# Seven quarter products for the second layer of one more piece, with GpSimd as a second choice for the sums of weights and x

## The chip, the cores and the metric

The kernel runs on one core of a Trainium2 chip. The metric is the device time of one execution in microseconds, as the median of several runs. A TensorE clock of 1.00 in a row of the profile is the full 2.4 GHz.

## The reference

Eight batches of eight heads attend over 576 tokens of 64 columns, under a mask that lets a block of 64 tokens see itself and earlier blocks. The result, seen as 4608 rows of 512 columns, goes through a feed-forward network with a hidden width of 2048.

```python
scores = scale * np.matmul(q, k.transpose(0, 1, 3, 2))
scores = np.where(block_i >= block_j, scores, -1e9)
attn = softmax(scores)
x = matmul(attn, v), as (4608, 512)
h = x @ w_in
g = h * np.clip(h + 3.0, 0.0, 6.0) / 6.0
return (g @ w_out).astype(np.float32)
```

## The kernel before

The 4608 rows are cut into 13 pieces, numbered 0 to 12; a late piece is 384 rows. A piece goes through the first layer in 16 steps of 128 hidden columns and then through the second layer. Attention of the pairs of heads that fill a piece comes before it; the last pairs (28 to 31) fill pieces 10 to 12.

Numbers are split into a high and a low 16-bit half, and a product of two such numbers takes three 16-bit products (high by high, high by low, low by high). Each matmul is done in two halves of 64 weight columns that run side by side; so the second layer of a 384-row piece is, for each of 16 hidden steps and each of 3 row tiles, 6 matmuls of 512 columns (`ffn2_`, tiles `g` and `o`).

In place of eight quarter products, a matrix product can be made of seven, if sums of quarters of both operands are formed first and the products are summed in a fixed way at the end. `STR = (10, 11, 12)` names the pieces whose first layer is done so: `w_comb` forms the sums of w_in (tiles `wr`, `wq`, result `ws`), `x_comb` those of x (tiles `xr`, `xt`), and `h_pair` makes the seven products of two hidden steps (a pair, `c` = 0 to 7, PSUM tile `m`) and adds them to `hf` by VectorE and ScalarE. `SO = (11, 12)` names the pieces whose second layer is done so as well: `t_comb` forms the sums of w_out (tiles `tr`, `tw`; results in places that `t_homes` lists), `g_pair` applies the activation and forms the four sums of g (tile `rs`; 16-bit results `gr`, `gs`), and `o_pair` makes the seven products into six PSUM banks; at the end 14 additions by VectorE form the output rows (`osb`). A product of `o_pair` is 6 matmuls of 256 columns and 6 of 128.

For a piece in `SO` the products of the first layer have only two PSUM banks (the pool `ps_h`) after the first two pairs of `SO[0]`; a piece in `STR` alone takes three of five from another pool (`bank` in `h_pair`).

The instructions are recorded first (`Recorder.add`), some of them with several engines to choose from. `ORDER`, a packed table, then gives the order of all steps and the engine of each; each engine works through its own list in that order, and waits where an operand isn't ready. `SLOTS` tells which buffer of a pool a tile takes. In the kernel before, the sums of g and w_out may be made by VectorE or GpSimd, those in `w_comb` and `x_comb` by VectorE alone, but for the additions of the two 16-bit halves (`plus`).

Line 423 of the profile is the helper that emits every step, so that rows are told apart by their tiles.

Of the kernel before, what the change touches and what calls it, by code (L numbers as in the profile page):

```python
# [56 lines left out]
SO = (11, 12)  # L57
# [1883 lines left out]
```

## Time and profile before

| | |
|---|---|
| median of 3 runs | 951.19 us (949.94 to 953.29) |
| profiled execution | 951.95 us, span 950.2 us |
| instructions | 34711 |
| TensorE busy | 942.8 us, 99% of the span |
| VectorE busy | 860.0 us, 91% |
| ScalarE busy | 722.0 us, 76% |
| GpSimd busy | 98.3 us, 10% |
| mean granted clock | 0.999 |

The time of an execution is the span and 1.75 us around it. Busy shares are means over the whole execution; stages differ. Durations in rows are those of single instructions, and neighbours on an engine overlap a little, so that a sum of durations is more than the busy time. A busy TensorE is not necessarily at its peak rate, since matmuls are pipelined: what a matmul costs in a stream is read from the distance between starts.

### The profile page before, as it was taken

The numbers are of one execution on the slowest core, as the hardware profiler recorded it, in microseconds if no ns is written. First come the engines' busy times: TensorE is split into PE (matmuls) and PEld (weight loads), VectorE is DVE, ScalarE is ACT, GpSimd is POOL, SyncE is SP. The second block draws the span as 40 slices with busy tenths as digits, with TensorE's granted clock in tenths as the row PEclk, the third lists the DMA queues.
The fourth block names the chain that finished last, engine by engine and source line by source line (L and its number), as shares of the span: only waits on it lengthen the run. The fifth ranks groups of instructions, "written<-read, shape, count | busy, mean of one in ns | idle before, by whom it ended". The sixth has DMA issues, their size and how long they took to land.

```text
span 950.2 us, 34711 instructions
## 1 busy us (share of the span) xinstructions
PE 942.8 (99%) x14108; PEld 686.3 (72%) x14108; DVE 860.0 (91%) x2526; ACT 722.0 (76%) x1791; POOL 98.3 (10%) x283
## 2 busy tenths in 40 slices
PE   9999999999999999999999999999999999999998
PEld 7777777766677766666667666666666667789998
DVE  5988999999999999999999999999899998999987
ACT  6989898888988878888788878778665356676662
POOL 1443101100000000110000010100000102000000
PEclk9999999999999999999999999999999999999999
DMA  7877699989999999999999899986785000000001
GB/s 211 280 246 213 125 178 169 180 166 181 167 189 168 179 188 162 183 189 181 165 201 181 169 165 180 179 162 121 127 128 106 2 2 36 2 35 4 14 26 36
DMA packets 390704, 132.93 MB, mean 140 GB/s; under 512 B 373264, under 2 KB 376592, under 8 KB 390544
## 3 DMA queue, kind: packets, MB, share of 16 engines
q1 hardware_dynamic: 389456, 129.87, 71.7%
q8 instruction: 110, 1.80, 0.8%
q10 hardware_dynamic: 1088, 0.85, 0.3%
q14 instruction: 50, 0.41, 0.1%
HBM read 45.09 MB, written 9.44 MB: 57 GB/s over the span
## 4 chain that ended last, share of the span: by engine, by line
PE 97%; DMA 1%; DVE 1%; ACT 0%; issue 0%; SPq 0%; DVEq 0%
PE o L423 37%; PE h L423 30%; PE m L423 9%; PE s L423 7%; PE pv L423 6%; PE pf L423 1%; PE sf L423 1%; PE pt L423 1%; DMA qkT<-qks 1%; PE pr L423 1%; PE gm L423 0%; DMA qf<-in_q_dram 0%; PE warm L423 0%; PE o_1b L423 0%; PE o_2b L423 0%; PE o_0b L423 0%
## 5 line engine op out<-in xcount | busy, mean ns | idle before, releaser
L423 PE MATMUL o<-wout,g 128*64 128x512 f16 (+2 forms) x2760 | 346.5, 378 | 0.0
L423 PE MATMUL h<-x,win 128*64 128x384 f16 (+2 forms) x3568 | 330.1, 318 | 0.0
L423 PEld LDWEIGHTS <-win 128*64 128x64 f16 (+1 forms) x4432 | 231.7, 110 | 81.3 <-issue 1.7
L423 PEld LDWEIGHTS <-g 128*64 128x64 f16 x2784 | 154.0, 110 | 98.6
L423 DVE SCALAR_TENSOR_TENSOR phl<-p,st,phl 128x64 f16<-128x64 f32 (+4 forms) x364 | 154.9, 447 | 4.2 <-ACT phl L423 2.3
L423 ACT ACTIVATE p<-p,st 128x192 f32<-128x192 f32 (+8 forms) x252 | 139.1, 553 | 22.7 <-DVE st L423 20.7
L423 DVE CUSTOM_DVE_ANT_0 p<-s,none,esc 128x64 f32<-128x64 f32 (+7 forms) x252 | 119.9, 486 | 14.6 <-PE s L423 11.2
L423 ACT ACTIVATE r<-h,eg,sh 128x384 f32<-128x384 f32 (+1 forms) x176 | 101.5, 591 | 40.2 <-PE h L423 33.9
L423 ACT ACTIVATE phl<-p,st 128x512 f16<-128x512 f32 (+5 forms) x173 | 97.2, 582 | 11.2 <-DVE st L423 6.1
L423 PE MATMUL s<-qkT 128*64 128x512 f16 (+7 forms) x1120 | 98.5, 287 | 0.8 <-DMA qkT<-qks 0.8
L423 DVE SCALAR_TENSOR_TENSOR g<-r,g 128x384 f16<-128x384 f32 (+1 forms) x160 | 86.2, 546 | 3.8 <-ACT g L423 3.0
L423 DVE SCALAR_TENSOR_TENSOR r<-r,eg,h 128x384 f32<-128x384 f32 (+1 forms) x144 | 84.2, 586 | 5.8 <-ACT r L423 4.5
L423 ACT ACTIVATE g<-r 128x384 f16<-128x384 f32 (+1 forms) x117 | 58.3, 503 | 18.2 <-PE o L423 11.3
L423 PEld LDWEIGHTS <-qkT 128*64 128x64 f16 x1120 | 53.4, 110 | 25.1 <-DMA qkT<-qks 1.0
L423 PEld LDWEIGHTS <-vhl 128*64 128x64 f16 x1344 | 58.4, 110 | 13.4
L423 PE MATMUL pv<-pT,vhl 128*64 128x192 f16 (+2 forms) x1344 | 67.2, 233 | 0.0
L423 ACT ACTIVATE hf<-m 128x192 f32<-128x192 f32 x90 | 28.5, 327 | 36.9 <-PE m L423 31.9
L423 PEld LDWEIGHTS <-ws 128*64 128x64 f16 x1152 | 52.0, 110 | 4.1
L423 ACT ACTIVATION_READ_ACCUMULATOR p<-p,st 128x1 f32 x252 | 47.7, 189 | 0.0
L423 DVE SCALAR_TENSOR_TENSOR qks<-qk,rs_q,qks 128x576 f16<-128x576 f32 x56 | 46.8, 838 | 0.9 <-ACT qks L423 0.6
L423 PE MATMUL m<-x,ws 128*64 128x192 f16 x864 | 46.8, 246 | 0.0
L423 PE MATMUL m<-x,win 128*64 128x192 f16 x768 | 41.4, 246 | 0.4 <-DVE hf L423 0.4
(229 smaller groups left out, 1414.1 us busy)
## 6 DMA issues: line engine op xcount, KB each, us to landing
vx<-vhl SPq DMA_DIRECT2D x56, 160.0 KB, 3.4
vnat<-in_v_dram SPq DMA_DIRECT2D x63, 128.0 KB, 3.5
qk<-in_k_dram SPq DMA_DIRECT2D x28, 288.0 KB, 4.4
qk<-in_q_dram SPq DMA_DIRECT2D x28, 288.0 KB, 3.9
out_dram<-osb SPq DMA_DIRECT2D x29, 256.0 KB, 2.8
rawo<-in_moe_w_out_dram SPq DMA_DIRECT2D x13, 512.0 KB, 4.9
x<-in_moe_w_in_dram SPq DMA_DIRECT2D x9, 512.0 KB, 5.5
rawi<-in_moe_w_in_dram SPq DMA_DIRECT2D x6, 512.0 KB, 4.8
```

The lines of the kernel that those rows point to most:

```text
L423: getattr(eng, method)(*args, **kw)
```

## The change

Piece 10 joins `SO`. So its 288 matmuls of 512 columns in the second layer become 672 (8 pairs, 7 products, 6 matmuls of 256 columns and 6 of 128), its activation goes through `g_pair`, its products of the first layer have two PSUM banks from the third pair on, its outputs are summed by 14 additions of VectorE, and `t_comb` comes before piece 10 in place of piece 11. Since part of the place for the sums of w_out is still in use then (x of piece 10 lies in `vall`), nine of the twelve blocks that lay there move into longer `ws` tiles. The subtractions in `w_comb` and `x_comb` may now be made by GpSimd, and `wr` is made in two halves of 512 columns. The order table and the slot table are new; the order is as before up to the attention of pair 26, where TensorE is in the second layer of piece 7.

```diff
-SO = (11, 12)
+SO = (10, 11, 12)
...
+    def minus(out, a, b):
+        nc.add([(e, "tensor_tensor", (out, a, b), dict(op=ALU.subtract)) for e in ("vector", "gpsimd")])
+
     def w_comb(c):
-        r = attp.tile([P, NDT, NH], F32, tag="qks", bufs=1, name=f"wr{c}")
-        plus(r, win[:, c, :, 0], win[:, c, :, 1])
+        wr = [ffp.tile([P, 2, NH], F32, tag="stage", bufs=NST_B, name=f"wr{c}_{j}") for j in range(2)]
+        for j, r in enumerate(wr):
+            plus(r, win[:, c, 2 * j:2 * j + 2, 0], win[:, c, 2 * j:2 * j + 2, 1])
...
-        nc.vector.tensor_add(o[:, 0], a21, a22)
-        nc.vector.tensor_sub(o[:, 1], o[:, 0], a11)
-        nc.vector.tensor_sub(o[:, 2], a11, a21)
-        nc.vector.tensor_sub(o[:, 3], a12, o[:, 1])
+        plus(o[:, 0], a21, a22)
+        minus(o[:, 1], o[:, 0], a11)
+        minus(o[:, 2], a11, a21)
+        minus(o[:, 3], a12, o[:, 1])
...
-        t = pool.tile([P, 4, 2, 2, P], F16, tag=tag, bufs=bufs, name=f"ws{c}")
+        nu = 2 if tag in ("qkT", "pT2") else 1 if tag == "pT01" else 0
+        t = pool.tile([P, 8 * 2 * P + nu * 2 * DM // 2], F16, tag=tag, bufs=bufs, name=f"ws{c}")
+        more[c] = t[:, 8 * 2 * P:].rearrange("p (i l n) -> p i l n", i=nu, l=2) if nu else None
...
     def x_comb(pc):
-            nc.vector.tensor_sub(t1, b12, b11)
-            nc.vector.tensor_sub(t2, b22, t1)
-            nc.vector.tensor_sub(t3, b22, b12)
-            nc.vector.tensor_sub(t4, b21, t2)
+            minus(t1, b12, b11)
+            minus(t2, b22, t1)
+            minus(t3, b22, b12)
+            minus(t4, b21, t2)
...
     def t_homes():
-        va = vall.rearrange("p v j h d -> p (v j h d)").bitcast(F16)[:, :4 * 3 * 2 * NM]
-        va = va.rearrange("p (c i l n) -> p c i l n", c=4, i=3, l=2)
+        va = vall.rearrange("p v j h d -> p (v j h d)").bitcast(F16)[:, :3 * 2 * NM]
+        va = va.rearrange("p (i l n) -> p i l n", i=3, l=2)
-        rest += [[va[:, i]] for i in range(4)]
+        rest += [[more[3], more[5]], [more[4], va[:, :1]], [more[6], va[:, 1:2]], [more[7], va[:, 2:]]]
```

In `ffn_step` the block that calls `t_comb` stands after the one that calls `x_comb` and `w_comb`.

How the table moves the work shows at two places. The first is the list of GpSimd behind the attention. In a row, the operation stands with its output, an arrow and its inputs; `rs10_2` is the sum tile of pair 2 of piece 10. Before, these are all the sums that GpSimd makes, for pieces 10 to 12 together:

```order
L423 TENSOR_TENSOR xr10_2_2229<-x2_83 128x384
L423 TENSOR_TENSOR xr10_1_2232<-x2_83 128x384
L423 TENSOR_TENSOR wr2_2242<-win_85 128x1024
L423 TENSOR_TENSOR xr11_2_2353<-x3_84 128x384
L423 TENSOR_TENSOR wr7_2257<-win_85 128x1024
L423 TENSOR_TENSOR tw0_2330<-tr0_0_2328 128x256
L423 TENSOR_TENSOR tw0_2330<-tr0_1_2329,tr0_0_2328 128x256
L423 TENSOR_TENSOR tr1_0_2331<-wout_86 128x512
L423 TENSOR_TENSOR rs12_3_2469<-hf12_3_2466 128x192
L423 TENSOR_TENSOR rs12_3_2469<-rs12_3_2469,hf12_3_2466 128x192
```

After, two pairs of piece 10 alone:

```order
L427 TENSOR_TENSOR rs10_2_2324<-hf10_2_2315 128x192 x2
L427 TENSOR_TENSOR tw4_2286<-tr4_0_2284 128x256
L427 TENSOR_TENSOR tw4_2286<-tr4_1_2285,tr4_0_2284 128x256
L427 TENSOR_TENSOR tw4_2286<-tr4_1_2285,tw4_2286 128x256
L427 TENSOR_TENSOR rs10_2_2324<-rs10_2_2324,hf10_2_2315 128x192
L427 TENSOR_TENSOR rs10_2_2324<-hf10_2_2315,rs10_2_2324 128x192
L427 TENSOR_TENSOR tw4_2286<-tr4_1_2285,tw4_2286 128x256
L427 TENSOR_TENSOR rs10_3_2331<-rs10_3_2331,hf10_3_2328 128x192
```

Ten sums of GpSimd have become 146, and 64 of them stand between the first sums of piece 10 and the first of piece 11; none of the sums that add the two halves of w_in, w_out or x (`wr`, `tr`, `xr`) is left there.

The second place is VectorE's list at the sums of g. Before, in piece 11, where the sums of w_out were still made:

```order
L423 TENSOR_TENSOR rs11_3_2395<-hf11_3_2392 128x192
L423 SCALAR_TENSOR_TENSOR hf11_4_2399<-rs11_4_2402,eg8_698,hf11_4_2399 128x768
L423 TENSOR_TENSOR tw5_2345<-tr5_1_2344,tw5_2345 128x256
L423 TENSOR_TENSOR rs11_4_2402<-hf11_4_2399 128x192
L423 SCALAR_TENSOR_TENSOR gs11_3_1_2398<-rs11_3_2395,gs11_3_1_2398 128x384
L423 SCALAR_TENSOR_TENSOR gr11_4_2403<-hf11_4_2399,gr11_4_2403 128x576
L423 TENSOR_TENSOR tw5_2345<-tr5_1_2344,tw5_2345 128x256
L423 SCALAR_TENSOR_TENSOR gs11_3_0_2397<-rs11_3_2395,gs11_3_0_2397 128x384
```

After, in piece 10, where that now falls:

```order
L427 TENSOR_TENSOR hf10_3_2328<-m10_3_7_2329,hf10_3_2328 128x192
L427 SCALAR_TENSOR_TENSOR gs10_1_0_2313<-rs10_1_2311,gs10_1_0_2313 128x384
L427 TENSOR_TENSOR hf10_3_2328<-m10_3_8_2330,hf10_3_2328 128x192
L427 SCALAR_TENSOR_TENSOR gs10_1_1_2314<-rs10_1_2311,gs10_1_1_2314 128x384
L427 TENSOR_TENSOR win_85<-tw4_2286,win_85 128x2x128
L427 TENSOR_TENSOR tr5_0_2287<-wout_86 128x512
L427 SCALAR_TENSOR_TENSOR hf10_3_2328<-rs10_3_2331,eg8_698,hf10_3_2328 128x768
L427 TENSOR_TENSOR ws3_2251<-tw4_2286,ws3_2251 128x2x256
L427 TENSOR_TENSOR rs10_3_2331<-hf10_3_2328 128x192
```

The sums themselves (`rs`, `tw`) are gone from VectorE but for one; the residuals that wait for them (`gs`, `win`, `ws`) stay, and now wait for GpSimd.

## Rows read from the trace of the kernel before

**Rows 1.** The page, busy time, share of the span and instructions of each engine.
```profile
PE 942.8 (99%) x14108; PEld 686.3 (72%) x14108; DVE 860.0 (91%) x2526; ACT 722.0 (76%) x1791; POOL 98.3 (10%) x283
```
**Rows 2.** The page, chain of work that ended last, share of the span by engine.
```profile
PE 97%; DMA 1%; DVE 1%; ACT 0%; issue 0%; SPq 0%; DVEq 0%
```
**Rows 3.** Waits of TensorE: waiting and releasing work, us in total, times, longest.
```profile
PE m L423 <- DVE hf L423: 0.4, 1, 0.4
```
**Rows 4.** Chain that ended last: start us, us, work, count of matmuls.
```profile
729.48 3.88 PE o L423 x36
...
764.27 1.95 PE h L423 x24
...
775.52 1.98 PE m L423 x48
...
931.80 14.02 PE o L423 x336
```
**Rows 5.** TensorE's timeline, second layer of piece 11: start us, us, operation, count.
```profile
869.86 0.36 PE L423 MATMUL o<-win,gs 128*64 128x128 f16 x6
870.03 0.36 PE L423 MATMUL o<-wout,gr 128*64 128x128 f16 x6
...
871.51 0.85 PE L423 MATMUL o<-vnat,gs 128*64 128x256 f16 x12
872.17 0.69 PE L423 MATMUL m<-x,ws 128*64 128x192 f16 x12
```
**Rows 6.** Stretch 860 to 880: us, busy PE, PEld, DVE, ACT, POOL, clock, DMA, GB/s.
```profile
860.00:880.00 20.00, 20.00 (x485) 19.85 (x481) 19.14 (x45) 13.51 (x29) 0.00 (x0) 1.00 0.02 4
```
**Rows 7.** VectorE by form, 700 to 950: count, busy us, mean ns of one, idle before.
```profile
L423 DVE TENSOR_TENSOR hf<-m,hf 128x192 f32<-128x192 f32 x72 | 24.5, 353 | 10.0 <-PE m L423 7.5 <-ACT hf L423 1.3 <-ACT gs L423 0.5
L423 DVE SCALAR_TENSOR_TENSOR g<-r,g 128x384 f16<-128x384 f32 x35 | 20.9, 605 | 1.5 <-ACT g L423 1.3
L423 DVE SCALAR_TENSOR_TENSOR gs<-rs,gs 128x384 f16<-128x384 f32 x32 | 17.6, 552 | 0.1
L423 DVE SCALAR_TENSOR_TENSOR hf<-rs,eg,hf 128x768 f32<-128x768 f32 x16 | 16.2, 1015 | 0.4 <-ACT rs L423 0.4
L423 DVE SCALAR_TENSOR_TENSOR gr<-hf,gr 128x576 f16<-128x576 f32 x16 | 12.0, 752 | 0.0
L423 DVE TENSOR_TENSOR ws<-wq,ws 128x1024 f16<-128x1024 f32 x8 | 10.8, 1354 | 1.4 <-ACT ws L423 1.4
L423 DVE TENSOR_TENSOR tr<-wout 128x512 f32<-128x512 f16 x15 | 10.2, 686 | 0.0
L423 DVE TENSOR_TENSOR wq<-wr 128x256 f32<-128x256 f32 x16 | 6.6, 419 | 0.1
```
**Rows 8.** VectorE's timeline from 743 to 745: start us, us, operation.
```profile
743.19 0.62 DVE L423 SCALAR_TENSOR_TENSOR r<-r,eg,h 128x384 f32<-128x384 f32 x1
743.72 0.35 DVE L423 SCALAR_TENSOR_TENSOR x<-pv,x 128x192 f16<-128x192 f32 x1
743.99 0.42 DVE L423 TENSOR_TENSOR wq<-wr 128x256 f32<-128x256 f32 x1
...
744.71 2.37 DVE L423 SCALAR_TENSOR_TENSOR g<-r,g 128x384 f16<-128x384 f32 x1
```
**Rows 9.** GpSimd's timeline from 640 on, sums only: start us, us, operation.
```profile
744.49 2.18 POOL L423 TENSOR_TENSOR wr<-win 128x1024 f32<-128x1024 f16 x1 [13.52 <-DVE wq L423]
...
796.78 1.58 POOL L423 TENSOR_TENSOR tw<-tr 128x256 f32<-128x256 f32 x1 [8.34 <-DVE ws L423]
798.32 0.73 POOL L423 TENSOR_TENSOR tw<-tr,tr 128x256 f32<-128x256 f32 x1
...
911.20 0.71 POOL L423 TENSOR_TENSOR rs<-hf 128x192 f32<-128x192 f32 x1 [110.86 <-DVE hf L423]
911.99 0.60 POOL L423 TENSOR_TENSOR rs<-rs,hf 128x192 f32<-128x192 f32 x1
```
**Rows 10.** VectorE's timeline beside the sum at 798.32: start us, us, operation.
```profile
798.40 0.93 DVE L423 TENSOR_TENSOR tw<-tr,tw 128x256 f32<-128x256 f32 x1 [0.62 <-POOL tw L423]
```

More of the change, by code (lines that the diff above doesn't have):

```diff
@@ new lines @@
+    "p4IhxXHv^{rKGOupEdg+ZS(G`+?zM{)At>E`!4OkhV3>-@7%p@Yj=Ff+QTQ-&6#`a9~Srh_m3S0XU{$SHR;d!d-or_H#|mpH2H{)"
+    "^#$_hi(jS~eZAUnZOfId+n)cmHNKSb?Zfr-%QmBZUc7weyL8#|*WPb_5=j05c%nyO=8$<GF&2Kdo|bm@4xj8qVu>UDq}5}u;UlF("
+    "6B8J+z+q1I&hc(k6Q)Z#&D1@v>GY{HC52B14W9ZWIE%-bpYco-lx!v`6^|;Ll&xKv*&H%CLRU0}Un~%^S+3kMV~>Ql)Q(HZiySe2"
+    "!mOlJ)z#d^`2|72OVV<p)DzpIr>#0LJ0|wHW==!Xbm_I$wx!MG6`^OtLPD1<-_UV==dRs1PE=OO&BHpoSI8B;UDX>m?eD9pn>^#i"
+    "-1?rzmoxi`r#IJIo;;=a{b%Z#gYzCWTs(U0@!!wq&R@9n<msWqQ~upFFuWZ9^~(HbMql2}h=2Zi!JfU!Z?E31S>3ZXA+fe@o$;;p"
@@ new lines @@
+    "7AB^R^zCnceq?Ohx@E_AvmZ$<zhrJqmwhBkYumKj?eE=LR#@|UpFD<mjvnfO!<Uo|`Y_Ycxpb1(tUGsyj~G1i{wNIG5gjW!ov8h@"
+    "AE?f*T-BSKx6mJopp_4cOJMu1_VEi)YY1fPU42&*lZGXy<nO*#P?$V_Ph`{rZP(HC>9N-rEj*ri<JgIcw4$uavHYqD<Ht?ZZMwW="
+    "Yc{94rg-y}h!NjX_wLL1&WpKtX^iWdwL2bmpIW#6<hJN1-2Ff1@PD38J$UHM&bjjrANlqB&)@AMZ}V>6db{Y|oedlR-OagGw&dRZ"
+    "_YWREdK|IXh>>mm;YQA+DXv_$U}^5qyg?3*gNH;itpkQRIX^w1Ft8CUV_o)*64r`@`2~gM;!%^IxkxychIF^1Sv8>;>apd|O=+^v"
+    "I4iRk7FhgnKMw-&=Evh-KDlp-9_>xC8E^a5lYBKG@Z~G7;XbjA^J8B72ff)`CtWyU;>j__!69LGV=4Aq#>H)DN@-EAdcS(j+BVHB"
@@ new lines @@
+    "leBcZ=Bc;u)Nh?O{qD{TKc#A0QTgjD>oTt{IB{=%NyYt#r_Y={w;}vd<(0=(t$!P;H?}`{dj6lmu4i&x))2!7Mwkn`J2Lkfcg{BM"
+    "GU=Xi*=*9}o+(pJOfO#Qn`v>%^11okW7GCbzcy#D=^(4Y`>{9=GjsBRAqNlPJ&V1DQ+yA{k>Zb^IJt<Boul<Ra&*L-w;x94=H(A9"
+    "FM_|9ckhdBol1MZRTO%!xBu|*w2rv=Q-a5+9YYHehozG#{nj?zq|X?O?@PXvc%^0h`Z`av5uQ8nN0uzx?qF-DOiAruF>ChdmClaT"
+    "C6;qa-8R*KFZ=PE=Kk~7(yB$%rt|nJIzu32o^q+4ySnoCyoDFSe~kV4=em}?c`--5WvkVeKOYZb*Wfh~kx@;}{sGZ3<0drx9p5$o"
+    "V&H;HMzR0KG%h#Tuy$QbO|5HCUGSm9>$eect!*8hggr;joMkQBxMF2*U-w|Dp?}DXdp)Z*ZMI)I$T{%b`G&oYjZNqo=MYBP`t-TO"
@@ new lines @@
+    "zMc0U$oD^d@#t~8(>7)CGsVQ2S=rlnFn2YFz7BU`i#V@T8rI7<yWhU^9C08AE=~*WiTr)nr_W!$7Hy}yeo(L&T<x{%H)31cZr-|m"
+    "C&H2Uv3=>Xk)s@SQT)!Z^&RWJ$=o7i#*7wAy>|&D1;WA&gQCa!_}+i#w`cH>yKlPps_(j&l<wQPJ9XUnp;xa>;C%XAQJFTes=B6j"
+    "e_U@ydR<b_jOAsMhRy8nn^m72fA8?*BbQgKTK)ES!j#z$=B0d@GxzKD8wYOAzxCwlpMwh)K6}1K^5W%Uscg{_H^a4g`2|$^Uw6ha"
+    "xWzts6c!CXen|K2q4U2Vna^Y39e(xt#L<(dnD9VPEWLDQMC^Ckx%00LjGV|6Yn!t_e;JSZ{6!ma;qse{E<3z^CQsS26*tx7(N|Be"
+    "Z)1)9wi!i^G!3(~`d(W%W|FO4!^*~D`>0iB(T{6N@I?Qz(^t$_zx{z7?HllJP0L!0MPSvmjUm6*&8^;aqW))S(EjO!rr+i12mS{C"
@@ new lines @@
+    "lPf1wRJL!PXmY2u^RDT=Hj-<{!9&e|y1Hk~TQD}=Y`&sr;o&1s$HgB{nDr(u_WlFzLxb|(nSJ^XJMs9F&lV*nB`;oLx72>w@>33u"
+    "9%nqghOgfczG#JE20K+Mdt#0`dhGqML4#A%mMqO4@#rijYuWPIIoB7T{_yxh=D8JfmMpbew$kFG^ZARHE?XGAwluzS!|&Ej6E<fg"
+    "&NA(72mY$5|Fx7{C$TGTOdGeqy+guV7`S~0aTL~Uqd7dJMSMZDRRA`GKpH~aLlFjt;>UT9pRj!5wY`L)R9ZNl!F(5I?HhDE$vtJ?"
+    "_4xO4n=r*7Wdu29^oPMijZCIaQxz0Wj4jf+_^^`Q%8N^;bnZA~yK;47*G|o($sc?B&Z|qyc6IMwHFM3{F;x}Q6DlJUZ(OQge5<DR"
+    "a$VD^{^nV$ubf@9_U4QsJ;t|g?-@0F&Zm|O^<3WEz4I=fyLzo5BXi-JE$l;w@7*}EZ{4=6>>N(+&G`%V%Vl}%j*g8|C~x06w)J?p"
@@ new lines @@
+    "fZuxm?!nVS)kC!iZtG3>M~|mWe{$f|NUdv>Sn}=VRL!gC?fGfxQa6vMBcGjckNN(i@@MQAujel|Umrc~f#I*=Co@Lf_00Ue#lYcD"
+    "#c1zaB(vLO%I2)GKIK*8CuCQ9n~$(|WNjGtaM&FuXJ4v|jcwe*jf?93{`2u|*j5kUIkv_pgx1tHHrv^6qCIYH+P>q_Ge7#yUHkU0"
+    "2wdEjm;|3^jIbc);oy+xk?Zf>FDNY16~`weCMPAAMBF*pT3FQ9p3`yk)iI|B$4_YUI=fm@Uc5}@6Y_KSOx}I>08x{Y+DjtuegA=~"
+    "J0kc<dmZR}@>Fohn@K(MOX+<x%b2In^v^Oi3wZmE;Sxj<hK8NBUT}_ezFVpN^!e+B*>mPz44-lH3y;m=`_B_Zf4d}iu)^9XT)*Ei"
+    "v^TI*3CAdGBd%OkUc0XT@pICU$fyYu+b0)u2i-48`!%K195Z%&%($u3e*dv3i+xybnVylEmA!M<p6RndSM+z@e6i&8nGydADk>kv"
@@ new lines @@
+    "-Fr~qu%M}`xy3@-8s6z8bK6@zbhq8Gr_X9156^d3sh8mJ8jmO1eKk4z&CD@Zmo7Vd;NTI@<wsXotXy?&^|9A8&tLeQyKeo4LtPtf"
+    "w?A(?{HyWzn>A~XpWJ>TYSZQyFC$+?=l%KnukKWPM|VtYXP3d-cYWL5f8Vk-0(bq#7yF@K@r3>zA3xFPmu(#`61!(O4!%JeGtSZ~"
+    "M<o9C;b+g-UNU9kc!~6q%nfUu>%s6`!n7IYe$~|2)p@B4D`C{=L3#OuovsYAbGSLkYxsoegNKyI$0d%KG19vr$%l9AcHy05d&dgj"
+    ")U=ecNkh|DuU+F;z05zr1YM6QQzsAWaWb4at+KASs@K_w8+Msi-_Y0Cxgs#AgSwJ^@X+DcHAjxFTVLMP9DHmKXItO$w;Sc9wf(c+"
+    "Tnm}KYEI~eP1MbM_dR&{Ve$T*tb21y*i#=pK0fb#@tK7)cb#oHw`J?Q?c0iUoa^T=?EZV=&Z3W>KJWNvV0iIT!jr_iUy>Q$zTZ9Y"
@@ new lines @@
+    "^~X=9EBDmzlfSy2-hk)0?w*8Ks&OeUF)A}YJ&7-%yU#DcNS{5ouv}mj=phO!D6DmZ&yYV?6iVy+)55VY!jdN2*bxb&qAA_t8Mvvt"
+    "h_6)l%_y>G!UvCf)^1o|_tL!H)7n2JHBF7Nsj6;xvRSiEyK#C&dAiq|;f<TNY~5jE8og~hNlxA!@GvtYD_f<md~Q49Wq-|!2@^+-"
+    "_8ax8Hz(rlyIGM@k7H)<oU_OK_1t;ypYHYfF#n71xbZIg*sKLV;+mSje*f0e%3Zi<ar=^GOGp09|MYqJsL^d5AAfmsT!p{sjQDU5"
+    "O#kdTe-<r1y^3dH$>b{qGM~OPxt`sBMQ-jAU-8UYsTp3wt#JRybJM3`4fC@7de-1qq^V}CUU@6)wl*SjUQTYosdJH0MOka34UDG8"
+    "s5N<7dk4pp`MQ$%#o2`mVk7Ph8nSfRs=>>jNjtmtA2=9&ekg%>0(U4jYRtkhr<bh29*$Xg<mlK38{vD+`MayHnytBa|KZqi<NY?R"
@@ L233 @@
[L233 removed]
+    "c-l>t2XZ7a3<H_||7H^nYR7wZH9;B%5P;m(75mGKirh<vF4cOhd&tp_sM^=wlNGazwYS4}`)~9uA1Gv}BG>LvsMrsunhn}AyD2va"
+    "QKL6e>1l7MV6Vlys8JmKR3fjs`S4<?2p(puQ?^}ndP==KMNMibUDPg3|N0F&yY^!1ET<pkz29zCg6g5h`_3stC3pE-(g?bFt!SeP"
+    "bpig7x^vsx*X<R$0aR@bfZWR#3W_R<WkE@LPeUPYMcFrHv>Ov>0=GTj2JWtTHBpr^w<&OwRQr?dgcp@v?yQZNa&GzLCrDDn?0|?x"
+    "UuuRf@@U2#&4~kDriTKz!P(*%nR?DNj%@%RZtg<x)D^5m^FROysMXh5rTZv@qT%NwP{EI2(2#~n!w8pJYABvavc*XAB;F|9<;FL{"
@@ L234 @@
+    ")mp-wRq+RJ{0YG"
 )
@@ L1299 @@
     sw = {}
+    more = {}
     homes = []
@@ L1453, in t_comb @@
         o = attp.tile([P, 4, NM], F32, tag="phl1", bufs=1, name=f"tw{c}")
-        def minus(out, a, b):
-            nc.add([(e, "tensor_tensor", (out, a, b), dict(op=ALU.subtract)) for e in ("vector", "gpsimd")])
         minus(o[:, 0], b12, b11)
@@ L1746, in ffn_step @@
             pc, f = divmod(done1, NFT)
-            if pc == SO[0] and f == 0:
-                was = nc.key, nc.cls, nc.grp
-                nc.cls = "a"
-                homes.extend(t_homes())
-                for c in range(NCH):
-                    nc.grp = 3200 + c
-                    t_comb(c)
-                nc.key, nc.cls, nc.grp = was
             if pc in STR and f == 0:
@@ L1765, in ffn_step @@
                         w_comb(c)
+                nc.key, nc.cls, nc.grp = was
+            if pc == SO[0] and f == 0:
+                was = nc.key, nc.cls, nc.grp
+                nc.cls = "a"
+                homes.extend(t_homes())
+                for c in range(NCH):
+                    nc.grp = 3200 + c
+                    t_comb(c)
                 nc.key, nc.cls, nc.grp = was
```

264 lines of the change are left out of this document (112 added, 152 removed).

## The prediction

> **What bounds the kernel now.** I read the page first. TensorE is busy for 942.8 of 950.2 us, VectorE for 860.0, GpSimd for 98.3 [rows 1], and the chain of waits that ended last runs over TensorE for 97% [rows 2]. The waits confirm it: in the part that the change touches, TensorE waited once, 0.4 us, for VectorE's additions to `hf` [rows 3]. So TensorE's stream of matmuls is the bound, and what the change is worth is the time that it takes out of that stream, less the new waits that it puts in. The second engine to watch is VectorE: in the densest stretch it is busy for 19.14 of 20 us while TensorE loses nothing, 20.00 of 20 [rows 6]. Thus 96% of VectorE is still covered here, and there is little room above it.
>
> **TensorE's part.** It loses 288 matmuls of 512 columns. In a stream, 36 of them take 3.88 us [rows 4], 0.108 each, so 31.0 us go. It gains 56 products of 6 matmuls of 256 and 6 of 128 columns. The distance of starts is 0.17 for six of 128 columns and 0.66 for twelve of 256 [rows 5], so a product takes 0.33 + 0.17 = 0.50 and 56 take 28.0. The closing block agrees: 336 matmuls in 14.02 us [rows 4], or 28.0 for 672; its last matmul's run-out of some 0.2 us counts twice in that, so 27.6 is as likely. By counted columns alone (seven for eight of 31.0) the gain would be 3.9. I take **3.2 us**, with 3.0 and 3.9 as the ends. The added 384 weight loads lie in these rows already, since the products of pieces 11 and 12 have them too.
>
> **Banks and outputs.** Products of piece 10's first layer now turn in two PSUM banks, and piece 10 hands six banks to piece 11 where it handed three. Pieces 11 and 12 do both today, and TensorE's one wait there is 0.4 us [rows 3]. I put 0.2 on piece 10, at most 1. The 14 output additions and the wider `g` work are VectorE's and count below. The copying of outputs at the end of the program is the same as before and costs nothing new. Moving `t_comb` from piece 11 to piece 10 makes pieces 11 and 12 lighter and piece 10 heavier; the time is decided in piece 10.
>
> **VectorE and GpSimd in piece 10.** Take the stretch of the new order from the last product of pair 0 of piece 10 to that of pair 0 of piece 11. TensorE has there 56 groups of first-layer products, 49 groups of six matmuls of 256 columns, 46 of 128, 29 of 512, and 5.5 hidden steps of piece 9. At 1.98 / 4, 0.33, 0.17, 3.88 / 6 and 1.95 us [rows 4, 5] these take 27.7 + 16.2 + 7.8 + 18.8 + 10.7 = **81 us**.
>
> VectorE has 137 instructions in it. By rows 7: 24 additions to `hf` at 0.353 (8.5 us), 8 activations at 1.015 (8.1), 14 `gs` at 0.552 (7.7), 7 `gr` at 0.752 (5.3), 26 of 512 columns at 0.686 (17.8), 20 of 256 at 0.42 (8.4), 13 `g` and `r` of piece 9 at 0.6 (7.8), 4 `ws` at 1.354 (5.4), and 21 smaller ones, 9.9 together at the means of their kinds. That is 78.9. Neighbours overlap: the one at 743.19 lasts 0.62 and the next starts 0.53 later, then 0.35 and 0.27 [rows 8]; with 0.08 off each, 68 us remain. Without GpSimd's help that would be more by the 64 sums that the new table gives it there, 27 of `g`, 9 of x and 28 of the weights, some 0.3 each: 19 us, 87 in all, which can't be covered by 81. So the help isn't an ornament; it is what lets piece 10 join.
>
> GpSimd's price: 0.71 and 0.60 for 192 columns, 0.73 for 256 [rows 9], so 36 x 0.66 + 28 x 0.73 = 44 us of the 81. GpSimd itself has room. The question is what its sums cost VectorE while they run. At 744.49 GpSimd began a long sum and VectorE's `g`, normally 0.6, took 2.37 [rows 8, 9]; at 798.32 a sum of 0.73 stretched VectorE's `tw` from 0.42 to 0.93, by 0.51 [rows 7, 9, 10]. But the sum at 796.78 was itself the one that waited (1.58 in place of 0.73), and the two at 911 cost VectorE nothing [rows 9]. So of the four short sums, 3.62 us long, VectorE lost 0.51: **0.14 us per us** of GpSimd. These are the same operations at the sizes that the change moves, so I take that; the ends are 0 and 0.51 / 0.73 = 0.7, the price when VectorE stands in the way each time. With 0.14, VectorE needs 68 + 6 = 74 of 81 us, 91%, below the 96% that is covered today. In pieces 11 and 12 it gets lighter than now.
>
> What speaks against this is told by the Trainium skill, "SBUF — State Buffer", section "Who interferes with whom": VectorE's second SBUF operand comes through a read port that it shares with GpSimd, and whichever comes second waits for the whole of the other's instruction. The trace agrees at 744.49 and at 798.32. Taken strictly it makes the 0.7 the rule and the 0.14 an accident of few rows.
>
> **The sum.** Against the profiled execution: 951.95 - 3.2 + 0.2 = 948.95 us (its span 950.2 becomes 947.2). That execution is 0.8 above the median of the runs, 951.19. From the median I forecast **948.2 us**. Less than 0.3% (2.85 us) can hardly be told from no change, so the forecast of 3.0 lies just beyond it.
>
> **Rivals.**
> 1. GpSimd holds VectorE up, and VectorE bounds piece 10. Of its 68 us there, all but the 24 additions to `hf` and the 6 `r` of piece 9, which read PSUM, have both operands or a whole operand in SBUF: about 85%. A price of 0.7 x 0.85 = 0.6 per us adds 26 us: 94 against 81, so TensorE would wait up to 13 us, and 3.0 would be the gain against it. The next bound is then VectorE's list, not GpSimd's. Some of it is made good, since TensorE's list runs ahead of the late pairs by some 5 us and piece 11 is lighter: 948.2 + 8 to 13 = 956 to 961. It decides from (81 - 68) / 44 = 0.3 per us on. For it: the row at 798.32, and that GpSimd works for half of the stretch. Against it: the rows at 796.78 and 911, where VectorE lost nothing.
> 2. Half of that. At 0.37 per us, midway between 0.14 and 0.6, VectorE needs 84 us, TensorE waits 3, and the gain is used up: 951 us, within 0.3%. The long sum at 744.49 speaks for it, the short ones don't.
> 3. The chain from first-layer product to `gs` has grown by two or three sums on GpSimd, at 0.65 for 0.35 each, some 1 us with the handovers. In the new order the first second-layer product of a pair stands 38 us of TensorE work (columns counted at 2.4 GHz) behind its last first-layer product for pair 0 of piece 10, but only 4.6 and 5.0 for pairs 6 and 7; the chain (0.35 for the addition, 1.0 for VectorE's activation step and, as an estimate from that row, as much for ScalarE's on the same 768 columns, 0.75 for `gr`, then the sums) needs 4 to 5. If it is late at both, 1 to 3 us go: 949 to 951.
>
> **How the numbers follow.** The forecast gets 0.45: its own range is 947 to 949.5, and runs spread by 3 us, so I count 0.33 of it as faster by over 0.3% and 0.12 as the same. Rival 1 gets 0.27, all slower. Rival 2 gets 0.18, of it 0.16 the same and 0.02 faster. Rival 3 gets 0.10, half faster, half the same. That makes 0.40 faster, 0.33 the same, 0.27 slower. The range that holds 8 in 10 runs from 946.5 (the gain by columns, and a little from a lighter VectorE) to 957.5, where the upper part of rival 1 is left out.
>
> **What would show it.** In the new profile: 672 `o` matmuls of piece 10 in place of 288, at 0.50 us a product; GpSimd busy for about 190 us in place of 98; VectorE's total about the same or less; TensorE's waits still under 1 us in all behind the start. Rival 1 is right if VectorE stands at 98% or more between the first products of piece 10 and of piece 11, its `gs`, `tr` and `ws` rows are longer than in rows 7, and TensorE shows waits for `hf` or `gs` there; the forecast is wrong then. If TensorE waits for GpSimd's `rs` by way of `gs` at pairs 6 and 7 alone, it is rival 3. If the products take more than 0.52 us, the first term is wrong.

## The result: slower, 962.5 us for a forecast of 948.2

The changed kernel takes **962.54 us** (median of 4 runs, 960.5 to 965.0), the kernel before in the same session 952.24: the ratio is 1.0111 with a 95% interval of 1.0078 to 1.0145. The forecast said 948.2 with a range to 957.5; rival 1 had said 956 to 961, by the mechanism that the runs below show as the main one.

The profiled execution of the changed kernel has a span of 961.0 us. Page, busy time (answers to [rows 1]) and chain of work that ended last (to [rows 2]):

```profile
PE 943.8 (98%) x14492; PEld 710.5 (74%) x14492; DVE 872.1 (91%) x2450; ACT 721.2 (75%) x1794; POOL 209.8 (22%) x416
...
PE 83%; DVE 8%; DMA 5%; ACT 1%; issue 1%; SPq 1%; POOL 0%; DVEq 0%; ACTq 0%; POOLq 0%
```

VectorE has 76 instructions fewer and is busy for 12 us longer; 8% of the chain now runs over it, and 0% over GpSimd. Waits of TensorE (to [rows 3]; us in total, times, longest):

```profile
PE o L427 <- DVE gs L427: 5.8, 4, 4.1
PE pv L427 <- DMA pT<-phl: 1.8, 1, 1.8
...
PE pv L427 <- DVE st L427: 0.8, 1, 0.8
PE m L427 <- DVE hf L427: 0.5, 2, 0.3
```

The 4.1 us are one wait, for `gs` of pair 5 of piece 10. The wait for `pT` lies at 324.9 us, far ahead of the change.

Stretches (to [rows 6]; us, then busy time of PE, PEld, DVE, ACT, POOL, then clock, DMA share, GB/s):

```profile
720.00:740.00 20.00, 19.51 (x264) 13.96 (x262) 20.00 (x29) 10.67 (x21) 16.03 (x18) 1.00 0.28 67
...
800.00:820.00 20.00, 17.99 (x416) 16.93 (x413) 20.00 (x26) 9.96 (x22) 15.58 (x17) 1.00 0.01 2
820.00:840.00 20.00, 15.83 (x330) 14.74 (x326) 19.96 (x30) 9.51 (x19) 17.21 (x19) 0.91 0.01 3
840.00:860.00 20.00, 19.91 (x464) 19.10 (x461) 19.56 (x36) 13.94 (x34) 13.15 (x17) 1.00 0.01 2
860.00:880.00 20.00, 20.00 (x497) 20.00 (x494) 17.97 (x43) 10.35 (x23) 4.23 (x6) 1.00 0.16 43
```

Where GpSimd works for 15 us of 20 or more, VectorE is full, with only 26 to 30 instructions in 20 us (45 in [rows 6]), and TensorE loses 0.5 to 4.2 us of 20. Where GpSimd has 4 us, VectorE has room and TensorE is whole. VectorE by form from 700 to 962 (to [rows 7]; count, busy us, mean ns of one, idle before):

```profile
L427 DVE SCALAR_TENSOR_TENSOR gs<-rs,gs 128x384 f16<-128x384 f32 x48 | 31.5, 661 | 0.5 <-ACT gs L427 0.2
...
L427 DVE TENSOR_TENSOR hf<-m,hf 128x192 f32<-128x192 f32 x72 | 23.6, 349 | 9.7 <-PE m L427 8.3 <-issue 0.8 <-POOL rs L427 0.2
L427 DVE SCALAR_TENSOR_TENSOR gr<-hf,gr 128x576 f16<-128x576 f32 x24 | 22.7, 947 | 0.1
...
L427 DVE TENSOR_TENSOR tr<-wout 128x512 f32<-128x512 f16 x16 | 13.1, 826 | 0.0
```

Against [rows 7], `gs` went from 552 to 661 ns, `gr` from 752 to 947, `tr` from 686 to 826: all three have both operands in SBUF. The addition to `hf` takes one operand from PSUM and stayed (353, now 349). The timeline of VectorE and GpSimd at 807 to 811 us shows one such knot (start us, us, operation):

```profile
806.86 1.11 POOL L427 TENSOR_TENSOR wq<-wr,wr 128x256 f32<-128x256 f32 x1 [0.63 <-DVE ws L427]
...
807.30 1.28 DVE L427 SCALAR_TENSOR_TENSOR gr<-hf,gr 128x576 f16<-128x576 f32 x1
...
807.93 1.24 POOL L427 TENSOR_TENSOR wq<-wr 128x256 f32<-128x256 f32 x1
...
808.51 0.94 DVE L427 TENSOR_TENSOR wq<-wq,wr 128x256 f32<-128x256 f32 x1
```

GpSimd starts at 806.86 beside VectorE's `tr` and takes 1.11 us instead of 0.73; `gr` starts at 807.30 and takes 1.28 instead of 0.75; the next GpSimd sum takes 1.24 beside `gr`, and VectorE's `wq` (0.42 in [rows 7]) takes 0.94 beside that one. Each engine stretches the other.

Both lists grew, so which of them decides? From 808.5 to 839.1 us the chain that ended last runs over VectorE alone, up to a first-layer product; GpSimd isn't in it (some of its pieces: start us, us, work):

```profile
808.51 0.94 DVE wq L427
809.45 1.47 DVE gs L427 x2
...
819.53 0.80 DVE gr L427
...
827.00 1.00 DVE ws L427
828.00 0.73 DVE vnat L427
...
838.34 0.47 DVE xr L427
839.13 3.43 PE m L427 x72
```

**Where the 10.8 us of span came in.** The order of work is the same up to product 12 of piece 7. VectorE's `r` of that product starts at 592.2 us before and 593.5 after; that of product 0 of piece 9 at 688.0 and 691.2. That cuts the span in three: start-up, 592.2 against 593.5 (+1.3); the middle, 95.8 against 97.7 (+1.9); the **last part**, 262.2 against 269.8 (+7.6). The first is scatter: in the 15 kernels below, alike up to there, it lies between 589.9 and 594.9. So below I give each kernel's median, but read causes from the last part and from **piece 10's stretch** (from the end of VectorE's last work on the first-layer products of pair 0 of piece 10 to that of pair 0 of piece 11). Both come from one profiled execution of each kernel, so 1 or 2 us between two of them are no finding.

### The profile page after: what moved, and what is told of

It reads as the page before. It is cut to its first block, busy times and chain, and to the rows that moved or that the text cites. A ratio compares the mean times of both kernels' runs of the same rounds, so it can differ in the third digit from the quotient of the medians.

```text
span 961.0 us, 35603 instructions
## 1 busy us (share of the span) xinstructions
PE 943.8 (98%) x14492; PEld 710.5 (74%) x14492; DVE 872.1 (91%) x2450; ACT 721.2 (75%) x1794; POOL 209.8 (22%) x416
## 4 chain that ended last, share of the span: by engine, by line
PE 83%; DVE 8%; DMA 5%; ACT 1%; issue 1%; SPq 1%; POOL 0%; DVEq 0%; ACTq 0%; POOLq 0%
PE o L427 31%; PE h L427 27%; PE m L427 7%; PE s L427 6%; PE pv L427 5%; SPq L427 1%; PE pf L427 1%; DMA pT<-phl 1%; PE sf L427 1%; DMA qr<-in_q_dram 1%; DVE hf L427 1%; PE pt L427 1%; DVE gs L427 1%; DMA x<-in_moe_w_out_dram 1%; DVE ws L427 1%
## 5 line engine op out<-in xcount | busy, mean ns | idle before, releaser
L427 PE MATMUL o<-wout,g 128*64 128x512 f16 (+3 forms) x2472 | 311.9, 378 | 0.0
L427 PEld LDWEIGHTS <-win 128*64 128x64 f16 (+1 forms) x4432 | 238.6, 110 | 74.2 <-issue 3.8
L427 PEld LDWEIGHTS <-g 128*64 128x64 f16 x2496 | 143.4, 110 | 86.0
L427 ACT ACTIVATE phl<-p,st 128x512 f16<-128x512 f32 (+5 forms) x179 | 100.3, 581 | 13.0 <-DVE st L427 6.6
L427 DVE SCALAR_TENSOR_TENSOR g<-r,g 128x384 f16<-128x384 f32 (+1 forms) x144 | 78.6, 554 | 2.3 <-ACT g L427 1.5
L427 POOL MEMSET p<- 128x64 f32 x112 | 16.4, 163 | 221.5 <-DVE phl L427 174.2
L427 ACT ACTIVATE g<-r 128x384 f16<-128x384 f32 (+1 forms) x107 | 52.8, 500 | 15.4 <-PE o L427 7.8
L427 PEld LDWEIGHTS <-gs 128*64 128x64 f16 x1152 | 52.8, 111 | 7.6 <-DVE gs L427 6.8
L427 POOL TENSOR_SCALAR st<-st 128x3 f32<-128x3 f32 x37 | 9.6, 259 | 194.4 <-ACT p L427 160.1
```

What stands on the lines that cost most here:

```text
L427: getattr(eng, method)(*args, **kw)
```

## The experiments

Theory A: GpSimd's sums hold VectorE up, and VectorE is the bound. Theory B: they cost it little and it is full anyway. Theory C (rival 3): the chain from first-layer product to `gs` is late, because GpSimd adds more slowly. All edits are to the changed kernel unless said.

### The sums given to VectorE

```diff
             o.eng = self.NAMES[hi // 32]
+            if o.eng == "gpsimd" and o.ways["gpsimd"][0][0] == "tensor_tensor":
+                name = o.ways["gpsimd"][0][1][0].tensor.name
+                if name:
+                    o.eng = "vector"
```

> The changed kernel with all 146 sums of GpSimd (rs, tw, wq, xt) given to VectorE at the same places of the order; GpSimd then has none in pieces 10 to 12. Theory A (GpSimd's sums hold VectorE up, about 0.55 us per us): in the stretch of piece 10 VectorE's list is 68 us plus 64 sums at 0.27, 85 us against TensorE's 81, in place of the 92 or so of the changed kernel, so 954 to 957 us in place of 962.5, and VectorE's gs at 0.55 and gr at 0.75 again. Theory B (the sums on GpSimd cost VectorE little, 0.14, and VectorE is full for some other reason): 19 us more of work less 6 us of holding up, 970 to 976. Theory C (the chain is late at pairs 6 and 7 because GpSimd is the slower adder): 2 or 3 us at most are won, 959 to 962, and the gs and gr rows stay as long as they are.

Measured: **974.9 us** (974.1 to 976.2), last part 283.8. The three others have another condition in the third line: `dst` between the first `rs10` and the first `rs11`, `name.startswith("rs")`, `not name.startswith("rs")`.

> Of the 146 sums only those between the first output of piece 10's rs and the first of piece 11's go to VectorE; pieces 11 and 12, and w_in's sums ahead of piece 10, keep GpSimd. Theory A, if the loss lies in piece 10's stretch: as the kernel with all sums on VectorE within 2 us, 954 to 958. If half of the loss lies in pieces 11 and 12 or ahead of piece 10: 958 to 960. Theory B: 968 to 974. Theory C: 959 to 962.

Measured: 965.45 us, last part 275.6.

> Of the 146 sums the 70 of rs (pieces 10 to 12) go to VectorE, the 76 of the weights and of x stay with GpSimd. It takes GpSimd out of the chain from first-layer product to gs. Theory A: 27 sums of 0.27 us more for VectorE in piece 10's stretch, 7 us, against 18 us of GpSimd's sums at 0.43, 8 us: within 3 us of the changed kernel, 960 to 965. Rival C (GpSimd in the chain is what is late): 3 us or more are won, 955 to 959.

Measured: 966.7 us, last part 276.6.

> The 76 sums of the weights and of x go to VectorE, the 70 of rs stay with GpSimd. Load theory: 37 sums in piece 10's stretch cost VectorE 12 us and spare it 11 of hold, some 13 more lie ahead of the stretch: 962 to 968 us. If the weights' sums on GpSimd are what makes the chain late (they share its list with rs): 956 to 961.

Measured: 970.65 us, last part 279.2. So, in this order of work, every split that takes sums back has a longer last part than the changed kernel (269.8). My expectations of theory A missed in all four, and 974.9 us lies where I had put theory B; what speaks against B comes with the copies below. I had put VectorE's list at 85 us without asking how well 85 can be packed beside 81. Piece 10's stretch, changed kernel and then all sums on VectorE (columns as in the stretches above):

```profile
752.40:843.50 91.10, 84.64 (x1552) 72.47 (x1550) 87.54 (x137) 49.91 (x102) 61.26 (x68) 0.98 0.03 11
```

```profile
756.00:853.80 97.80, 86.72 (x1558) 74.16 (x1554) 88.79 (x204) 49.58 (x102) 0.00 (x0) 0.97 0.03 10
```

VectorE is busy for 87.5 us with 137 instructions beside GpSimd, and for 88.8 with 204 alone. The 67 sums thus cost it about as much on GpSimd as on itself. I had put them at 6 us of VectorE's time on GpSimd and 19 on VectorE, a gain of 13; the gain is 1.3. GpSimd is the better place only since VectorE then idles less: 3.6 of 91.1 us against 9.0 of 97.8. Of these 9.0, 6.9 are waits for ScalarE, most of them for its rounding of sums just made. The order was made with the sums on GpSimd; one made for sums on VectorE was not tried. That `rs` back on VectorE is slower speaks against theory C as the main cause.

### The price by itself

In the kernel with all sums on VectorE, GpSimd makes each sum again into a tile that nobody reads (for which the constants of the attention, no longer used, give the space):

```diff
+            if o.copy:
+                self.nc.gpsimd.tensor_tensor(to, a, b, op=ALU.add)
```

> All sums on VectorE, and GpSimd makes each of the 146 a second time into a tile that nobody reads; nothing waits for GpSimd. What this adds to the kernel with all sums on VectorE is the bare price of GpSimd's sums. Theory A at 0.55 per us: 44 us of sums in piece 10's stretch cost a VectorE that is the bound there some 20 to 24 us, those of pieces 11 and 12 a few more, so 20 to 30 us on top. Theory B, 0.14: 6 us on top. Theory C: under 1 us on top.

Measured: **1020.7 us**, 45.8 above the kernel without copies, where theory A had 20 to 30 and theory B 6: over all 146 sums, some 100 us alone at the prices of the prediction, it is 0.46 per us. The same with GpSimd that almost only writes:

```diff
+                self.nc.gpsimd.tensor_scalar(self.spare[:, :3], first[:, :3], 1.0, 1.0, op0=ALU.mult, op1=ALU.mult)
+                self.nc.gpsimd.memset(self.spare, 0.0)
+                self.nc.gpsimd.memset(self.spare, 0.0)
```

> All sums on VectorE, and in place of each of the 146 GpSimd reads three numbers of the sum's first operand and then fills a tile of 256 columns twice (about 0.1 + 0.3 + 0.3 us, as long as a sum alone), nobody reads it. If it is GpSimd's reading of SBUF that holds VectorE up: under 3 us on top of the kernel with all sums on VectorE. If any work of GpSimd on SBUF does: as much as the copies, 20 to 30 us.

Measured: 979.5 us, 4.6 above, where I had allowed 3. Piece 10's stretch and VectorE's `gs` in it (by form), first with copies, then with writes:

```profile
766.00:886.50 120.50, 91.14 (x1558) 75.78 (x1554) 111.50 (x203) 49.57 (x102) 56.09 (x68) 0.93 0.02 8
```

```profile
L431 DVE SCALAR_TENSOR_TENSOR gs<-rs,gs 128x384 f16<-128x384 f32 x14 | 9.6, 689 | 0.7 <-ACT gs L431 0.6
```

```profile
754.90:852.70 97.80, 86.44 (x1558) 73.35 (x1554) 88.94 (x204) 49.70 (x102) 72.87 (x195) 0.97 0.03 10
```

```profile
L431 DVE SCALAR_TENSOR_TENSOR gs<-rs,gs 128x384 f16<-128x384 f32 x14 | 7.7, 550 | 0.9 <-ACT gs L431 0.8
```

The copies took VectorE from 88.8 to 111.5 us: 22.7 for the 44 us that the prediction gave these sums alone, **0.52 per us**. The trace counts 68 of them in the stretch where the prediction had 64; at its prices that is 47 us, and 0.48 per us. 72.9 us of GpSimd, 40.6 of them fills and the rest short reads, took it from 88.79 to 88.94: nothing. So it is the reading of SBUF that holds VectorE up; the 4.6 us of the writes are TensorE's waits for ScalarE's `hf` (11.1 us in place of 6.3), and ScalarE's `hf` waits 6.1 us for the short reads, whose tiles it has to write. This is the rule of the Trainium skill, "SBUF — State Buffer", section "Who interferes with whom": a VectorE instruction with two SBUF inputs contends with a GpSimd instruction that reads SBUF, and not with one that only writes it. Both halves hold here.

Does the price show where VectorE has some room? In the **kernel before**, the sums `rs` and `tw` of VectorE made a second time by GpSimd:

```diff
+            method, args, kw = o.ways[o.eng][0]
+            if o.eng == "vector" and method == "tensor_tensor" and args[0].tensor.name.startswith(("rs1", "tw")):
+                self.nc.gpsimd.tensor_tensor(self.spare[:, :args[0].shape[1]], *args[1:], op=ALU.add)
```

> The kernel before, with each of its 92 sums rs and tw that VectorE makes made a second time by GpSimd into a tile that nobody reads: some 62 us of GpSimd between 730 and 930 us, in a kernel whose TensorE waits for nothing there. VectorE has about 14 us to spare in these 200. Theory A at 0.5 us per us: 31 us more for VectorE, of which 14 hide: 960 to 972 us. At the price of the prediction, 0.14: 9 us more, all hidden, 950 to 953.

Measured: 974.2 us, ratio 1.0233 (1.0198 to 1.0267); 23 us, a little beyond theory A. The stretch of [rows 6] there:

```profile
860.00:880.00 20.00, 16.80 (x366) 15.24 (x362) 20.00 (x35) 9.85 (x21) 10.90 (x13) 1.00 0.01 2
```

VectorE does 35 instructions in place of 45, full, and TensorE loses 3.2 of 20 us. Nothing of piece 10's change is in this kernel.

### The sums left out

```diff
+            if o.eng == "gpsimd" and method == "tensor_tensor":
+                self.nc.gpsimd.memset(to, 0.0)
+                continue
```

> Leaves the 146 sums of GpSimd out altogether: GpSimd fills the sum's tile with zeros and reads nothing, so it neither holds VectorE up nor stands in the chain; VectorE, ScalarE and TensorE have the work of the changed kernel. If TensorE's saving of 3.2 us was judged rightly and all the rest of the loss is GpSimd's (hold, list and chain together): 947 to 951 us, one wait of TensorE for gs under 1 us. If part of the loss is VectorE's own order of work (gs of pair 5 behind the last chunk of w_out): a wait for gs of 2 us or more stays, and 951 to 955. If the change loses time ahead of piece 10 as well (between 600 and 650 us), 1 us stays there.

Measured: **954.6 us** (10 runs, 950.3 to 957.1), ratio 1.0017 (0.9996 to 1.0037), last part 260.4. Its stretch, and by the waits of TensorE the longest:

```profile
754.00:837.10 83.10, 81.27 (x1551) 72.72 (x1549) 68.20 (x136) 48.49 (x101) 16.86 (x70) 1.00 0.04 12
```

```profile
PE o L433 <- DVE gs L433: 1.6, 1, 1.6
```

This is the prediction's own working without GpSimd's price: TensorE 81.3 us (81 forecast) and VectorE 68.2 (68 forecast). The changed kernel's 87.5 less 68.2 is 19.3 us of hold, **0.44 per us** of the 44 (0.41 of the 47). The time itself lies where I had put "part of the loss is VectorE's own order", 951 to 955; that is tried in the next part. With only the weights' and x's sums left out, or only `rs` (a condition on the name in the first line):

> Leaves the 76 sums of the weights and of x out (filled with zeros, nothing read), keeps the 70 sums rs on GpSimd. Of GpSimd's 44 us in piece 10's stretch 18 remain, the hold falls from 18.7 to about 8 us, VectorE needs 77 of 81 us. Theory A: 950 to 954 us. If GpSimd's place in the chain to gs is what is late, however short its list: 956 to 960.

Measured: 955.95 us, last part 262.8.

> Leaves the 70 sums rs out (filled with zeros, nothing read), keeps the 76 of the weights and of x on GpSimd. If load decides (hold in proportion to GpSimd's time: 26 of 44 us stay, 11 us of hold, VectorE at 80 of 81 us): 956 to 959 us, with waits of TensorE of 2 to 4 us between 800 and 840. If the rs sums' place in the chain decides: 953 to 956, as with all sums left out.

Measured: 955.9 us, last part 264.7. Either half gives back most: 7.0 and 5.1 of the 9.4 us that both give. By the medians load and chain can't be told apart here, the floor of 954.6 is too near; I had put it at 950. The hold isn't spread evenly: VectorE needs 71.9 us in the stretch with only `rs` made, 3.7 above 68.2, and 81.0 with only the others made, 12.8 above. Per us that the sums take alone this is 0.2 and 0.4 to 0.5; why `rs` costs less was not tried.

Two forms between, with short reads that keep the chain's order (three numbers of each operand, then zeros), and with the first operand read whole:

```diff
+                for x in flat[1:]:
+                    self.nc.gpsimd.tensor_scalar(flat[0][:, :3], x[:, :3], 1.0, 1.0, op0=ALU.mult, op1=ALU.mult)
+                self.nc.gpsimd.memset(to, 0.0)
```

> Leaves the 146 sums of GpSimd out: in place of each, GpSimd reads three numbers of either operand and fills the sum's tile with zeros, so that the same tiles are written by the same engine at the same places and VectorE, ScalarE and TensorE have the work of the changed kernel. Theory A (the whole loss is what GpSimd's reading of SBUF takes from VectorE): VectorE's list in piece 10's stretch is back at 69 us, below TensorE's 81, and the time is what was forecast for a free GpSimd, 947 to 951 us; gs at 0.55 and gr at 0.75. Rival C (the longer chain at pairs 6 and 7 is the loss, the sums' hold is not): the chain stays within some 0.3 us a sum as long as it is, so 957 to 962. If TensorE's own saving was misjudged, VectorE is free and the time is still above 952.

Measured: 958.0 us, last part 266.0: in the range that I had given to rival C.

> Leaves the additions out in another way: each of the 146 sums of GpSimd reads three numbers of its second operand and then multiplies its first operand by one, over all its columns. GpSimd then reads one tile of SBUF in place of two, for about as long. If GpSimd holds VectorE up whenever it reads SBUF: 957 to 963 us, gs and gr about as long as in the changed kernel. If only its two-operand sums do: 947 to 952 us, gs at 0.55 and gr at 0.75.

Measured: 955.4 us, last part 264.0: between the two expectations. VectorE needs 68.3 us in the stretch with the short reads and 72.7 with one tile read: that holds it less than a sum, but it does. And yet TensorE waits once, 4.4 and 3.4 us, for `gs`. The chain of the second shows by what:

```profile
817.29 0.98 POOL tw L430
818.34 0.73 POOL tw L431
819.09 0.64 ACT ws L434
819.75 0.69 DVE ws L434
820.44 0.34 DVE vnat L434
820.78 0.48 DVE win L434
821.26 0.48 DVE gs L434
821.78 6.68 PE o L434 x116
```

Ahead of these lines the chain runs over GpSimd from 800 us on: its own list is full there (35.1 of 40 us), and VectorE's `gs` stands behind a `ws` that waits for it. The short reads show the same, with 5% of the chain over GpSimd: VectorE is as free as with no sum at all, GpSimd as busy as in the changed kernel (62.3 us), and yet the stretch takes 88.4 us in place of 83.1. So GpSimd's list is a second bound behind VectorE's: freeing VectorE alone leaves 5.6 of the 9.4 us of the last part.

### VectorE's order

`gs` of pair 5 stands behind the last chunk of w_out in VectorE's list. Three steps moved up:

```diff
+        late = [x for x in table if x[0] in (5821, 5822, 5823)]
+        table = [x for x in table if x not in late]
+        at = 1 + [n for n, _ in table].index(5852)
+        table[at:at] = late
```

> The changed kernel, all sums made, with three operations moved up in the order: VectorE's two gs of pair 5 of piece 10 and ScalarE's cast for the second stand ahead of the last chunk of w_out (wr, ws, vnat, win of chunk 7) and not behind it. If TensorE's wait of 4.1 us for gs is a matter of VectorE's order: that wait goes below 1.5 us, 957 to 960. If VectorE is simply full for the whole stretch, the wait comes back at the next place (hf or gs of pairs 6 and 7): 961 to 964.

Measured: 964.8 us, last part 271.7. The wait only moved, as its waits of TensorE show:

```profile
PE o L432 <- DVE gr L432: 3.3, 1, 3.3
...
PE o L432 <- DVE gs L432: 1.7, 3, 0.7
PE o L432 <- ACT gr L432: 1.4, 1, 1.4
```

> The kernel that fills the sums' tiles after short reads, with the same three operations moved up. VectorE is at some 79% there, so if its order is the cause of the wait of 4.4 us that was left, the wait goes: 951 to 954 us in place of 958. If GpSimd's list is the cause (it is busy for 34 of 40 us there), the wait stays: 956 to 959.

Measured: 958.6 us, last part 265.8 (266.0 without the move).

> All 146 sums left out (filled with zeros, nothing read), and the three operations on gs of pair 5 moved up ahead of the last chunk of w_out. If the order of VectorE's work is part of the rest: the wait of 1.6 us for gs goes and 952 to 954 us come out. If not, the wait moves to gr or gs of the next pair: 954 to 956.

Measured: 953.3 us (952.0 to 955.8), ratio 1.0032 (1.0020 to 1.0043), last part 262.5. The median lies where I had put "order is part of the rest", but against its own session's kernel before it is no faster than without the move (1.0017): in place of the wait for `gs` of pair 5 stands one of 2.0 us for `gr` of pair 6. In all three kernels moving these steps only moved the wait; another order was not tried.

## Why the prediction was wrong

- **TensorE's part: right.** The products run at 0.50 us where they run freely (0.33 + 0.16 from 833.30 on, last section), and the stretch took 81.27 us of TensorE, 81 forecast, once no sum was made.
- **VectorE's list: right in its own work, wrong in GpSimd's price.** This is the step that failed: "So of the four short sums, 3.62 us long, VectorE lost 0.51: 0.14 us per us". It should have been **0.44**, 19 us instead of 6, so VectorE needs 87.5 us and not 74. The four sums had been a bad sample [rows 9], as VectorE's timeline of the kernel before shows beside the first and the last two:

```profile
796.61 0.56 DVE L423 SCALAR_TENSOR_TENSOR g<-r,g 128x384 f16<-128x384 f32 x1
797.08 0.69 DVE L423 TENSOR_TENSOR tr<-wout 128x512 f32<-128x512 f16 x1
...
911.11 0.36 DVE L423 TENSOR_TENSOR rs<-hf 128x192 f32<-128x192 f32 x1
912.08 0.89 DVE L423 TENSOR_TENSOR hf<-m,hf 128x192 f32<-128x192 f32 x3 [0.61 <-PE m L423]
```

Beside the two at 911 VectorE had one short sum, begun first, then nothing from 911.5 to 912.08, and then additions to `hf`, which read PSUM; beside that at 796.78 it had begun first, and GpSimd waited. Only one in four held VectorE up, and that one cost 0.7 per us, the upper end. In the new stretch VectorE is busy for 87.5 of 91.1 us. The mean over few rows was taken from an idle neighbour and applied to a busy one.

- **"GpSimd itself has room": wrong where it matters.** The 44 us became 61.3, as VectorE holds GpSimd up too, and 32.8 of the 40 us from 800 on. GpSimd isn't in the chain of the changed kernel there, but it is as soon as VectorE is freed (the short reads).
- **"The help isn't an ornament": half wrong.** The sums cost VectorE about as much on either engine; GpSimd wins only by shorter idling. In this order what the change adds could not be hidden, whoever adds.
- **Rivals 1 and 2.** The mechanism of rival 1 is what happened (VectorE full, `gs`, `gr` and `tr` longer, waits for `gs`), at a price between its 0.6 and the 0.37 of rival 2. Its sign, VectorE at 98%, came out at 96% of the stretch (87.5 of 91.1 us) and at all of the time from 800 to 840. VectorE's 87.5 us stand 6.3 above TensorE's 81.3, and piece 10's stretch grew by 8.0, from 83.1 with no sums to 91.1; the other 1.7 aren't told apart. The point from which it decides, 0.3 per us, isn't borne out: with only the weights' and x's sums made VectorE needs 81.0 us, just TensorE's 81, and the last part is already 4.3 us longer than with no sums.
- **Rival 3** is there in small, and a pair earlier than it said: with no sum left TensorE still waits 1.6 us for `gs` of pair 5, or, after the move, 2.0 us for `gr` of pair 6. These waits run over VectorE, not over GpSimd's sums.
- **What no step had**: the middle part. It takes 95.8 and 96.1 us in the two kernels with the order of before, and 97.7 to 98.8 in all 15 with the new one, whatever their sums. The new order lets TensorE wait there in the attention (0.8 us for `st` at 628.6, 0.3 for a transfer at 604.8), where I had costed the moved work at nothing. Where the rest of the 1.9 us comes from, and why, was not tried.
- **The sum.** Last part: +9.4 for the sums, -1.8 for TensorE's gain less the wait that stays; middle +1.9; start-up scatter +1.3; together +10.8. (The -1.8 is the difference of 260.4 with no sums and 262.2 before.) So even with free sums this change would have been no gain: 954.6, ratio 1.0017.

No version here beats the kernel before.

## What to carry to other kernels

Work handed to GpSimd isn't free for a VectorE that is itself busy with two SBUF operands: here it cost VectorE 0.4 to 0.5 us for each us that the sums take alone (0.2 for `rs` by themselves), so compare such a price with what the work costs on VectorE. Take the price of a collision only from rows in which the two really met, and ask of each row what the other engine would have done in that time. Where a list must fit beside another, leave room for packing: VectorE's 88.8 us beside TensorE's 81 took 97.8. And when one engine is freed, ask which list stands next.

## What the runs showed of the hardware

GpSimd is held up as well. In the kernel that writes, its reads of three numbers took, by GpSimd's lines in piece 10's stretch (count, busy us, mean ns of one):

```profile
L441 POOL TENSOR_SCALAR spare<-tr 128x3 f32<-128x3 f32 x22 | 15.6, 708 | 3.1 <-DVE tr L431 1.3
L441 POOL TENSOR_SCALAR spare<-hf 128x3 f32<-128x3 f32 x17 | 7.1, 418 | 6.9 <-DVE hf L431 5.6
```

The same read took 0.20 us where it met nobody (820.74 in the kernel with short reads). And a wait can cost TensorE more than its length. TensorE's timeline of the changed kernel after the wait of 4.09 us (start us, us, operation, count):

```profile
829.59 0.79 PE L427 MATMUL o<-ws,gs 128*64 128x128 f16 x8 [4.09 <-DVE gs L427]
...
830.80 0.53 PE L427 MATMUL o<-win,gs 128*64 128x128 f16 x6
831.12 0.53 PE L427 MATMUL o<-ws,gr 128*64 128x128 f16 x6
...
833.30 0.49 PE L427 MATMUL o<-wout,gr 128*64 128x256 f16 x6
833.63 0.33 PE L427 MATMUL o<-wout,gs 128*64 128x128 f16 x6
833.79 0.38 PE L427 MATMUL o<-ws,gs 128*64 128x256 f16 x4
```

Six matmuls of 128 columns start 0.32 us apart, and 0.16 again at 833.6, where [rows 5] have 0.17: half speed, the lower of the clock's two levels (1.2 of 2.4 GHz; granted 0.73 on average from 828 to 832). From 829.6 to 833.3 that cost TensorE some 1.8 us on top of the 4.1, as an estimate from these starts; whether it lengthened the whole isn't shown, since the chain runs over VectorE until 839. Of the waits with fewer sums, those of 2.0 us (no sums, with the move) and 2.4 (only `rs` made) were followed by such a drop, with a granted clock of 0.60 and 0.57 from 824 to 828; those of 1.6 us (no sums) and 2.7 (`rs` left out) were not, with 1.00 in the four us behind them.
